# Beginning the first load from ScalarE's DMA queue instead of SyncE's

## The chip, the cores and the metric

The kernel runs on one core of a Trainium2 chip. A core has a matrix engine (TensorE, PE), three engines for elementwise work (VectorE or DVE, ScalarE or ACT, GpSimd or POOL) and SyncE (SP), which here only begins transfers. Transfers between the chip's memory and the core's on-chip memory are carried out by 16 DMA engines; an instruction on an engine's queue begins one. The metric is the device time of one execution in microseconds (us). Before the change the median of three runs is 224.49 us (224.32 to 224.66).

## The reference

Two blocks in a row, in float32. The first is a scan with decay: for 4 batches, 8 heads, 768 steps in chunks of 32, head width 32 and state width 16.

```python
log_a = np.log(np.clip(a, 1e-06, 1.0))
for c in range(nc):                       # chunks of 32 steps
    cum = np.cumsum(la, axis=-1)          # la: the chunk's log_a
    L = np.exp(cum[:, :, :, None] - cum[:, :, None, :]) * causal
    M = np.einsum('bhin,bhjn->bhij', Cc, Bc) * L
    y_intra = np.einsum('bhij,bhjd->bhid', M, xc)
    y_inter = np.einsum('bhin,bhnd->bhid', Cc, state) * np.exp(cum)[:, :, :, None]
    y[:, :, sl] = y_intra + y_inter
    state = decay_full[:, :, None, None] * state + np.sum(Bx, axis=2)
```

The second is a mixer on the result, laid out as 4 x 768 x 256: `u = x + (xt @ U @ V)` transposed back (rank 32, across the sequence), then `u + relu(u @ w_ch1) @ w_ch2` with 1024 hidden channels. U, V, w_ch1 and w_ch2 come in as float64 and are read as pairs of 32-bit words.

## The kernel before

The sequence of each batch is cut into three pairs of 128-step blocks, twelve pairs in all. One long hand-written list, PLAN, fixes the order of all steps on every engine; each word of it is a step and its numbers. In it, U0, B0, X0 and so on with a leading Y are loads begun early, A and K compute the decays, Q, T and V multiply and turn B and C, g, m and M make the masked products, n, j, i, s and u the scan itself, p and q the low-rank part, U, f, e, h and d the mixer's matmuls, c and R turn weight words into floats. F and the function `warm` put filler matmuls of the identity on TensorE (line 136), whose results nobody reads.

The kernel opens as follows. ScalarE loads the table of its activation functions (line 182). SyncE begins the load of `a` (line 186), 96 partitions of two rows of 512 bytes. Then helper constants are made on GpSimd and VectorE: the identity, triangles and the like (lines 301 to 332). TensorE runs a filler of 3 x 128 columns as soon as the identity is there, then turns `a` (line 343, `la_ps`), then another filler of 128 columns. VectorE clips the result (`la`, line 345), ScalarE takes its Ln (line 349). With the first words of PLAN, `YU0 c0 F3 YB0 A0 Q0.0 A1`, come the load of U's words, the start of their conversion, a filler of 3 x 128 columns, the first pair's B and C loads, and the decays: matmuls with `la` (lines 377 and 381), an Exp on ScalarE into F (line 384), and the product BC of B and C with F on VectorE (line 466, shown under the helper's line 174). F multiplies everything that follows.

All loads in PLAN go through `begin` (line 201), which uses the queue named by `issuer`. That is SyncE's queue, unless a word begins with Z, which then means ScalarE's; PLAN has no such word. SyncE works through its loads in order. Later ones (words B, X and w without a leading Y) are held until the last VectorE instruction written before them has ended (`hold`, line 194). The copy named `settled` (line 595) is a small VectorE instruction that keeps one group of matmuls behind another.

The diff touches the top level of the kernel's function. These are the lines in question, numbered as in the profile:

```python
182    nc.scalar.preload_act_table_set("natural_log_exp_and_others")
185    a_sb = const.tile([NB * NH * NC // 2, 2, P], FP32)
186    nc.sync.dma_start(
187        out=a_sb,
...
338    warm(3, "x")
343        nc.tensor.transpose(out=la_ps[:, g], in_=a_sb[:, g], identity=ident[:R, :R])
344    warm(1, "x")
```

Of the kernel before, what the change touches and what calls it, by code (L numbers as in the profile page):

```python
# [73 lines left out]
def kernel(  # L74
# [27 lines left out]
    nc = tc.nc  # L102
# [60 lines left out]
    class Kept:  # L163
# [6 lines left out]
        def __getattr__(self, name):  # L170
# [8 lines left out]
    vector = Kept(nc.vector)  # L179
    until = []  # L180

    nc.scalar.preload_act_table_set("natural_log_exp_and_others")


    a_sb = const.tile([NB * NH * NC // 2, 2, P], FP32)
    nc.sync.dma_start(
        out=a_sb,
        in_=a.rearrange("(g b) h (c s) -> g (b h c) s", g=2, s=P).rearrange(
            "g r s -> r g s"))

    x_sb, bc_sb = {}, {}
    pairs = [(b, q) for b in range(NB) for q in range(NPR)]
# [790 lines left out]
```

## Time and profile before

| | |
|---|---|
| median of 3 runs | 224.49 us (224.32 to 224.66) |
| the profiled execution | 224.41 us, of which the span from first to last instruction is 222.6 us |
| TensorE busy | 215.5 us (97%), 3022 matmuls |
| VectorE, ScalarE, GpSimd busy | 146.4, 108.7, 32.7 us |
| data moved | 14.59 MB by DMA, most of it in the first 60 us |
| issue of `a` on SyncE | at 0.81 us, 0.38 us long, landed 2.0 us after its start |
| issue of U's words on SyncE | at 1.24 us, 0.44 us long, landed 2.9 us after its start |
| ScalarE's table load | at 0.80 us, 1.28 us long |

In the rows of the profile, L186 is line 186 of the kernel, PE is TensorE's matmuls and PEld its weight loads, SPq the queue of SyncE's DMA instructions; `w<-ident,a_sb` means that the tile w is written from ident and a_sb, `x2` that two instructions are merged into the row. What stands in brackets is how long the engine was idle before it, and whose end released it. Ends of matmuls are modelled, their starts are recorded.

### The profile page before, as it was taken

What the parts mean: (1) busy time and instruction counts of PE and PEld (TensorE: products, weight loads), DVE (VectorE), ACT (ScalarE), POOL (GpSimd) and SP (SyncE); (2) the same over time, 40 slices, a digit from 0 to 9 for tenths busy, and PEclk for the clock granted to TensorE, in tenths of its full rate; (3) what the DMA queues carried; (4) which work ended last, traced back from release to release, by engine and by line L of the source; (5) the groups of instructions that cost most, each with busy time, mean ns of one, the idle gap of its engine ahead of it and who ended that gap; (6) DMA issues with size and microseconds to landing.
All of it is one profiled execution on the core that took longest, in us unless ns stands there. A gap on an engine that the chain in (4) does not pass through costs nothing.

```text
span 222.6 us, 7025 instructions
## 1 busy us (share of the span) xinstructions
PE 215.5 (97%) x3022; PEld 182.2 (82%) x3022; DVE 146.4 (66%) x314; ACT 108.7 (49%) x251; POOL 32.7 (15%) x44
## 2 busy tenths in 40 slices
PE   7999999999999999999999999999999999999994
PEld 4666566665668888889999996788999999999993
DVE  4688498568657755737955736959863955674921
ACT  3334745675668075543444214476535455553510
POOL 3012223405577053000010100000000000000000
PEclk9999999999999999999999999999999999999999
DMA  6968888898633446100120010000000100101011
GB/s 102 129 98 144 138 158 189 187 281 113 134 47 71 84 57 91 37 24 28 27 71 27 3 49 27 3 3 3 0 27 1 47 0 27 47 0 50 6 43 50
DMA packets 69520, 14.59 MB, mean 66 GB/s; under 512 B 63792, under 2 KB 67696, under 8 KB 69488
## 3 DMA queue, kind: packets, MB, share of 16 engines
q1 hardware_dynamic: 69488, 14.13, 32.3%
q8 instruction: 24, 0.39, 0.8%
q14 instruction: 8, 0.07, 0.1%
HBM read 10.98 MB, written 3.15 MB: 63 GB/s over the span
## 4 chain that ended last, share of the span: by engine, by line
PE 89%; DVE 5%; DMA 2%; SPq 2%; ACT 1%; issue 1%; POOL 0%; POOLq 0%
PE x L790 31%; PE z L790 24%; PE y L790 12%; PE y L680 3%; PE x L522 2%; PE y L642 2%; PE w L482 2%; DMA bc<-in_B_dram 2%; DVE M L174 2%; PE w L707 2%; SPq L202 2%; PE w L556 1%; PE x L136 1%; PE z L522 1%; PE w L734 1%; PE w L136 1%
## 5 line engine op out<-in xcount | busy, mean ns | idle before, releaser
L790 PE MATMUL z<-u,w 128*128 128x384 f32 x144 | 33.6, 347 | 0.0
L790 PE MATMUL x<-u,w 128*128 128x384 f32 x144 | 32.7, 344 | 0.5 <-DVE u L174 0.3
L174 DVE SCALAR_TENSOR_TENSOR words<-words 128x768 fp32r<-128x768 f32 (+3 forms) x35 | 29.5, 846 | 1.4
L790 PEld LDWEIGHTS x<-u,w 128*128 128x128 f32 x144 | 24.8, 188 | 1.8 <-DVE u L174 0.7
L795 ACT ACTIVATE x<-x 128x384 f32<-128x384 f32 (+1 forms) x30 | 13.6, 454 | 25.1 <-PE x L790 18.2
L790 PEld LDWEIGHTS z<-u,w 128*128 128x128 f32 x144 | 24.1, 189 | 0.9
L790 PE MATMUL x<-w2c,words 128*128 128x256 f32 x112 | 22.3, 339 | 0.0
L795 ACT ACTIVATE z<-z 128x384 f32<-128x384 f32 (+1 forms) x27 | 12.6, 466 | 18.6 <-PE z L790 18.6
L790 PE MATMUL y<-w,words 128*128 128x256 f32 x144 | 19.8, 283 | 0.0
L790 PEld LDWEIGHTS x<-w2c,words 128*128 128x128 f32 x112 | 18.3, 189 | 1.5
L174 DVE SCALAR_TENSOR_TENSOR words<-x,words 128x384 fp32r<-128x384 f32 x24 | 13.3, 554 | 9.3 <-ACT words L825 9.2
L790 PEld LDWEIGHTS y<-w,words 128*128 128x128 f32 x144 | 18.8, 190 | 0.3
L583 POOL TENSOR_TENSOR Sm<-S,own 128x256 f32<-128x256 f32 (+1 forms) x12 | 7.6, 634 | 76.4 <-DVE S L174 48.0
L174 DVE SCALAR_TENSOR_TENSOR words<-z,words 128x384 fp32r<-128x384 f32 x24 | 13.2, 552 | 5.2 <-ACT words L825 5.1
L825 ACT ACTIVATE words<-z 128x384 fp32r<-128x384 f32 x24 | 11.7, 491 | 10.1 <-PE z L790 10.0
L825 ACT ACTIVATE words<-x 128x384 fp32r<-128x384 f32 x24 | 11.8, 493 | 5.3 <-PE x L790 5.0
L790 PE MATMUL x<-w,words 128*128 128x256 f32 x96 | 14.2, 285 | 0.0
L790 PEld LDWEIGHTS x<-w,words 128*128 128x128 f32 x96 | 12.9, 190 | 0.2
L680 PEld LDWEIGHTS y<-M,x 64*32 64x32 f32 x768 | 8.1, 105 | 5.7 <-issue 3.0
L174 DVE TENSOR_TENSOR BC<-bc,F 128x512 f32<-128x512 f32 (+2 forms) x18 | 9.4, 535 | 4.7 <-DMA bc<-in_B_dram 3.2
L680 PE MATMUL y<-M,x 64*32 64x64 f32 x768 | 12.0, 223 | 0.4 <-DVE settled L174 0.3
L174 DVE SCALAR_TENSOR_TENSOR S<-S,kept,w 128x64 f32<-128x64 f32 x40 | 11.2, 279 | 1.6
(149 smaller groups left out, 411.9 us busy)
## 6 DMA issues: line engine op xcount, KB each, us to landing
words<-in_moe_w_ch_dram SPq DMA_DIRECT2D x7, 512.0 KB, 5.0
x<-in_x_dram SPq DMA_DIRECT2D x24, 128.0 KB, 3.7
out_dram<-ytok SPq DMA_DIRECT2D x24, 128.0 KB, 1.7
bc<-in_B_dram SPq DMA_DIRECT2D x24, 64.0 KB, 3.3
bc<-in_C_dram SPq DMA_DIRECT2D x12, 128.0 KB, 3.4
words<-in_moe_w_ch_dram SPq DMA_DIRECT2D x2, 256.0 KB, 3.8
words<-in_moe_U_dram SPq DMA_DIRECT2D x1, 192.0 KB, 2.9
words<-in_moe_V_dram SPq DMA_DIRECT2D x4, 48.0 KB, 2.8
```

What stands on the lines that cost most here:

```text
L136: nc.tensor.matmul(out=t[:, :m * P].rearrange("p (m i) -> p m i", i=P), lhsT=ident, rhs=ident[:, None, :].to_broadcast([P, m, P]), start=T ...
L174: self.last = call(*args, **kwargs)
L202: op = issuer[0].dma_start(**kwargs)
L482: nc.tensor.transpose(out=tp[:, i, v], in_=s["BC"][:, i, c + v].rearrange("p h n -> p (h n)"), identity=ident)
L522: nc.tensor.matmul(out=s["g"][r][cols, c], lhsT=s["T"][rows, 0, c, cols], rhs=s["Cm"][rows, :, :, ts(2 * c + p, Q)].rearrange("r v t i -> ...
L583: nc.gpsimd.tensor_tensor(out=s["Sm"][:, sl], in0=s["S"][:, sl].rearrange("p i (s d) -> p i s d", s=2), in1=own2[:, b, 4 * q + sl.start:4 ...
L642: behind["first"].append(nc.tensor.matmul(out=channels(k)[r // 2][ts(r % 2, H), c, p], lhsT=own[ts(r, Q)], rhs=st[k]["T"][ts(r, Q), 1, :, ...
L680: product = nc.tensor.matmul(out=y[n][ts(i, Q), c, p], lhsT=x_sb[k][half, c, h], rhs=s["M"][half, h // 2, c, h % 2], start=fresh(k, n, [i] ...
L707: nc.tensor.transpose(out=t[:, c, g], in_=yT[b][:, g, ts(2 * q + c, P)], identity=ident)
L790: nc.tensor.matmul(out=t, lhsT=lhsT, rhs=rhs, start=start, stop=True, skip_group_check=True)
L795: nc.scalar.activation(t, t, AF.Copy, scale=1.0 + EPS)
L825: nc.scalar.activation(gs[j, m // 2][0][:, m % 2], t, AF.Relu, scale=NEAR)
```

## The change

The load of `a` is begun by an instruction on ScalarE's queue, which stands ahead of ScalarE's table load. SyncE's queue, which had this load first, now begins with U's words. The order of all else on every engine is the same, and so are the data moved and the work computed.

```diff
-    nc.scalar.preload_act_table_set("natural_log_exp_and_others")
-
-
     a_sb = const.tile([NB * NH * NC // 2, 2, P], FP32)
-    nc.sync.dma_start(
+    nc.scalar.dma_start(
         out=a_sb,
         in_=a.rearrange("(g b) h (c s) -> g (b h c) s", g=2, s=P).rearrange(
             "g r s -> r g s"))
+
+    nc.scalar.preload_act_table_set("natural_log_exp_and_others")
```

## The prediction

> **What bounds the kernel now.** I read the page's busy shares first, then the timeline of the first 5 us with the DMA rows, then the chain of waits over the first 36 us, and last the rows where an engine waited for a load.
>
> From the head of the page, its busy times and its slices:
>
> ```profile
> span 222.6 us, 7025 instructions
> PE 215.5 (97%) x3022; PEld 182.2 (82%) x3022; DVE 146.4 (66%) x314; ACT 108.7 (49%) x251; POOL 32.7 (15%) x44
> PE   7999999999999999999999999999999999999994
> ```
>
> TensorE (PE) is busy for 215.5 of 222.6 us. All its idle time is 7.1 us, of which 1.43 us lies ahead of its first instruction. So a change that only hides work better can win little; one that makes PE wait early shifts all that follows.
>
> From the timeline of the first microseconds (start, length, what; in brackets the idle time before and its releaser), and then two rows of the DMA view (KB, median us from issue to landing):
>
> ```profile
> 0.80 1.28 ACT L182 ACT_TABLE_LOAD   x1 [0.80 <-PEq L967]
> 0.81 0.38 SPq L186 DMA_DIRECT2D a_sb<-in_a_dram  x1
> 1.24 0.44 SPq L202 DMA_DIRECT2D words<-in_moe_U_dram  x1
> 1.43 1.65 PE L136 MATMUL x<-ident 128*128 128x384 f32 x2 [1.43 <-POOL ident masks.py:199]
> 2.82 0.29 PEld L343 LDWEIGHTS w<-ident,a_sb 96*128 96x128 f32 x2 [0.89 <-DMA a_sb<-in_a_dram]
> 2.88 0.53 PE L343 MATMUL w<-ident,a_sb 96*128 96x96 f32 x2
> 3.98 0.36 ACT L349 ACTIVATE la<-la 128x192 f32<-128x192 f32 x1 [1.89 <-DVE la L174]
> ```
> ```profile
> words<-in_moe_U_dram SPq DMA_DIRECT2D x1, 192.0 KB, 2.9
> a_sb<-in_a_dram SPq DMA_DIRECT2D x1, 96.0 KB, 2.0
> ```
>
> The array a lands at 0.81 + 2.0 = 2.81, and its transposes start at 2.88, just when PE has done the filler matmuls of line 136. Both arrive together: an earlier a gives PE nothing, a later one makes it wait.
>
> From the chain of waits over the first 36 us:
>
> ```profile
> 1.43 1.65 PE x L136 x2
> 3.08 0.33 PE w L343 x2
> 3.40 0.48 PE x L136 x2
> 3.88 1.28 PE w L136 x2
> 5.16 0.64 PE w L377 x2
> ...
> 12.42 0.65 PE y L136 x2
> ...
> 19.61 4.09 DMA bc<-in_B_dram
> 23.70 0.02 issue
> 23.72 0.69 DVE BC L174
> 24.41 0.10 DVE settled L174
> ```
>
> Until 15 us the chain is PE, DVE and ACT, without a load after a; the first late load on it is a block of B, at 23.70. Two matmuls of 128x384 take 1.28 us at 3.88 and 0.65 us at 12.42: PE runs at half its pace at first, though the row of granted clocks shows 9 throughout.
>
> **The change part by part.** The sum is made against the profiled execution, 224.41 us: its span of 222.6 and 1.81 around it. It lies 0.08 under the median of the runs, 224.49.
>
> *Table load.* ACT and SP start within 0.01 us of each other (0.80, 0.81), so a's issue stays at about 0.80. I price it as SP's row: 0.38 us, and 0.43 to the next instruction (1.24 less 0.81). The table load moves to 1.23 and ends at 2.51. ACT's next work is the Ln at 3.98, which waits for DVE's la. That leaves 1.47 us of cover: cost nothing. Had the cover been under 0.43 us, the rest would have gone onto the chain through Ln.
>
> *a's landing.* What moves together with a changes. So far U's packets came behind a's, since U was issued 0.43 us later; now both queues start at once. In windows of 0.4 us from 1.80, 2.20 and 2.60 the DMA engines were 0.56, 0.59 and 1.01 busy at 159, 154 and 234 GB/s: while a moved, some 40% was free, and the full rate was 234. The best case is no delay (a still lands at 2.81; earlier is worth nothing). The worst is that U goes first and a lands only where U lands, 0.81 + 2.9 = 3.71: 0.9 late. Between them, with equal turns byte for byte, a's 96 KB go with 96 KB of U: 192 KB at 234 GB/s take 0.82 us, against 96 KB at about 157 GB/s, 0.61: 0.2 us late. I take 0.2, since the free share of the engines speaks for the near end.
>
> *What PE makes of it.* The cover is 0.06 us (weights at 2.82, matmul at 2.88); by the chain's modelled end of the fillers, 3.08, it would be up to 0.26. I take 0.06, as a start is measured and an end modelled. Behind the transposes PE has in its order the fillers at 3.40 and 3.88 and only then the decays of line 377, so these wait too although la is ready at 4.34: nothing there takes the delay up. After that the chain goes through ACT's Exp and DVE's BC, where PE's slow pace gives nothing back. So 0.2 - 0.06 = +0.14 us; ends 0 and +0.84.
>
> *SP's queue.* One issue goes: all SP loads may come up to 0.43 us earlier. The first one with a gate is the issue of w at 15.56, held by a BC product of DVE, which is done by about 15.2 (two of them run 14.94 to 15.56 and it is the first): so the lead past there is about 0.3, less what the delay of a takes from DVE. Who is waiting for these loads? No one before 20.52. From the timeline, the PE and DVE rows that wait for a load or follow it:
>
> ```profile
> 20.52 0.32 PE L556 MATMUL w<-x,BC 64*32 64x64 f32 x8 [0.26 <-DMA x<-in_x_dram]
> 23.72 0.69 DVE L174 TENSOR_TENSOR BC<-bc,F 128x512 f32<-128x512 f32 x1 [0.75 <-DMA bc<-in_B_dram]
> 23.76 0.45 PE L680 MATMUL y<-M,x 64*32 64x64 f32 x32
> 24.55 0.46 PE L680 MATMUL y<-M,x 64*32 64x64 f32 x32 [0.34 <-DVE settled L174]
> ```
>
> The wait at 20.52 is followed by one of 0.23 us for ACT's Vn at 21.07, so x earlier only lengthens the next wait. At 24.55 PE waits for the copy "settled", which stands behind BC on DVE but also waits for the products that PE ends at 24.21 (23.76 + 0.45); without the load it would start some 0.07 behind their end, as its copy at 19.09 does behind products ending at 19.02, so at 24.28 instead of 24.35. So 0.07 of the 0.34 is to be had. The DVE wait of 0.32 at 27.50 is covered, as its next M waits for PE's products ending at 28.6. I take -0.05. Ends: -0.60 (both waits of PE, 0.26 + 0.34, gone), and +0.8, as the landing of such a block differs by that much from load to load (4.09 on the chain, 3.3 in the median of B's loads), and a stream begun at another moment may fall worse; I stay near 0, since the block on the chain is already one of the late ones.
>
> *Around the span.* A second queue could cost at the end, where SP's queue waits 0.6 us in all for the other engines; ends 0 and +0.6, taken as 0, since ACT's own transfer is over 219 us before.
>
> Sum: 0.14 - 0.05 = +0.09 us: 224.50 for a run like the profiled one, and 224.6 beside the median of 224.49.
>
> **A page against it.** The windows show free DMA engines beside a, and the sum took equal turns from that. The Trainium skill, page "DMA: Bandwidth & Descriptors", section "Issuing engines are not separate DMA queues", says that starting transfers from several engines saves only the issuing time and that they interleave on the same engines; the section "Queues, rings and completion order" adds that the write that signals an end lands only after every earlier write of that engine, whatever its queue. By these, a's signal waits for U's packets that went ahead of it; in the extreme these are all of U's, and the sum would be 225.3, the first rival below, instead of 224.6. No run shown so far has two queues, so the trace decides nothing here.
>
> **The rivals.**
> - *a behind U (slower).* Place: the landing of a. The issue of U on SP is served first, or a's signal waits for U. a lands up to 3.71, PE waits 0.84: 224.49 + 0.84 - 0.05 = 225.3. It decides from a delay of about 0.55 on. For it: U has 768 pieces of 256 bytes against 192 of 512, and the engines are full from 2.6 on. Against: 40% free while a moves, and ACT starts 0.01 before SP. Chance 0.21.
> - *The loads' lead reaches PE (faster).* The waits at 20.52 and 24.55 both vanish: 224.49 - 0.60 = 223.9. It needs a to land in time, landings over 0.34 earlier, and ACT and DVE not to be next. Against: the rows of Vn and settled above. Chance 0.14, not all of it past the bound.
> - *The pace of PE (slower).* The half pace ends around 7 us. Should a gap at 2.9 put that off, the stretch from 7.2 to 11.0, with PE 3.39 us busy, would run at half pace: up to 3.4 us more, about half of it beside DVE's waits: 226.2. Against: PE is busy without a break from 3.1 to 7 in either case. Chance 0.04.
>
> **How the numbers follow.** My forecast, a small delay, has 0.61; its own range is 224.1 to 225.0. A measurement of this kernel can tell about 0.2% from no change, that is 0.45 us. Faster: 0.12 of the loads' lead and 0.01 of the forecast. Slower: 0.19 of a behind U, 0.04 of the pace and 0.06 of the forecast's own edge. The same holds 0.58. The range goes from 223.9 (the whole lead) to 225.4 (a behind U, a little over), leaving out the pace and part of the ends of the forecast.
>
> **What would show it.** In the changed profile: the issue of a on ACT's queue at 0.8 and the table load after it ending near 2.5; U issued at 0.8 on SP; a's time to landing (2.0 so far; 2.2 by my sum, 2.9 by the rival); the start of line 343 on PE (2.88 so far, 3.0 expected); the Ln about 0.14 later; the block of B near 23.70 landing up to 0.3 earlier with DVE's wait shorter and the PE row at 24.55 hardly moved. I am wrong if a lands where it did and PE still shifts, if ACT's issue takes much longer than SP's 0.38, or if the time moves by over 0.45 us with line 343 in its place: then it is in the loads after 15 us.

## The result and the profile after

The changed kernel takes 225.55 us in the median of four runs (225.35 to 225.68), the kernel before, now with a fourth run, 224.42 (224.32 to 224.66): a ratio of 1.0061, 95% interval 1.0046 to 1.0076. That is 1.13 us slower, where a time within 0.45 us of no change was held likeliest and 225.4 was the end of the range. The profiled execution took 225.48 us, 223.8 of it the span.

The timeline of the changed kernel's first microseconds, with the rows that answer to those shown of before (lines after 188 count one less than before):

```profile
0.80 0.45 ACTq L183 DMA_DIRECT2D a_sb<-in_a_dram  x1
0.81 0.42 SPq L201 DMA_DIRECT2D words<-in_moe_U_dram  x1
1.28 1.28 ACT L188 ACT_TABLE_LOAD   x1 [1.28 <-PEq L966]
1.43 1.65 PE L136 MATMUL x<-ident 128*128 128x384 f32 x2 [1.43 <-POOL ident masks.py:199]
4.12 0.29 PEld L342 LDWEIGHTS w<-ident,a_sb 96*128 96x128 f32 x2 [2.19 <-DMA a_sb<-in_a_dram]
4.12 0.58 PE L342 MATMUL w<-ident,a_sb 96*128 96x96 f32 x2 [1.05 <-DMA a_sb<-in_a_dram]
5.28 0.36 ACT L348 ACTIVATE la<-la 128x192 f32<-128x192 f32 x1 [2.71 <-DVE la L174]
```

And of its DMA view (KB, median us from issue to landing):

```profile
words<-in_moe_U_dram SPq DMA_DIRECT2D x1, 192.0 KB, 3.7
a_sb<-in_a_dram ACTq DMA_DIRECT2D x1, 96.0 KB, 3.3
```

The issue of a is where it was, at 0.80, but it lands 3.3 us later and no longer 2.0. TensorE has done its fillers at 3.08 and stands still for 1.05 us; the transposes begin at 4.12 instead of 2.88. U lands no earlier either: 0.81 + 3.7 = 4.5, against 1.24 + 2.9 = 4.1 before.

The chain of waits of the changed kernel shows what becomes of it:

```profile
0.80 3.27 DMA a_sb<-in_a_dram
4.08 0.05 issue
4.12 0.58 PE w L342 x2
4.70 0.48 PE x L136 x2
5.18 1.28 PE w L136 x2
6.46 0.64 PE w L376 x2
...
27.63 1.47 PE w L733 x12
...
33.46 1.53 PE z L789 x4
```

The last two rows stood in the chain of the kernel before as:

```profile
26.39 1.46 PE w L734 x12
...
32.22 1.53 PE z L790 x4
```

The chain now begins with the landing of a. The decays of the old line 377 start at 6.46 against 5.16 (1.30 later); the mixer's first matmuls of the old line 790 start at 33.46 against 32.22 (1.24 later); the span ends 1.2 later. TensorE's busy time is 215.5 us in both. So the whole loss is there after 4 us, and the rest of the kernel takes no more than about a tenth of a us of it back.

The packet records of the two traces part the 1.3 us of later landing. The end of a load is told by 16 signals, and it has landed with the last of them. Before, the first of a's 192 pieces of 512 bytes moved at 1.83 us, the last at 2.42, and the last signal came at 2.78. After, these are 2.24, 3.35 and 4.08. So 0.41 us is a later start, 0.52 (1.11 less 0.59) a slower run, and 0.37 (0.72 less 0.36) a later signal. U's first piece moved at 1.91: U, issued 0.01 us after a, was served before it. But a did not wait for all of U. Its first piece moved when 163 of U's 768 pieces had gone; then the two loads ran mixed, and a's last piece went before U's last (3.58), its last signal before U's (4.47).

### The profile page after: what moved, and what is told of

It reads as the page before. It is cut to its first block, busy times and chain, and to the rows that moved or that the text cites. A ratio compares the mean times of both kernels' runs of the same rounds, so it can differ in the third digit from the quotient of the medians.

```text
span 223.8 us, 7025 instructions
## 1 busy us (share of the span) xinstructions
PE 215.5 (96%) x3022; PEld 181.9 (81%) x3022; DVE 146.5 (65%) x314; ACT 108.6 (49%) x251; POOL 32.3 (14%) x44
## 4 chain that ended last, share of the span: by engine, by line
PE 91%; DVE 4%; DMA 1%; ACT 1%; issue 0%
PE x L789 31%; PE z L789 24%; PE y L789 12%; PE y L679 4%; PE y L641 3%; PE x L521 3%; PE w L481 2%; PE w L706 2%; PE w L555 2%; DMA a_sb<-in_a_dram 1%; DVE M L174 1%; PE z L521 1%; PE x L136 1%; PE w L733 1%; PE x L761 1%; PE w L751 1%
```

## The experiments

Two theories stood against each other at first: that U's load, begun at the same moment, holds a back (A), or that a first load from ScalarE's queue is slow in itself (B).

**U issued later.** The changed kernel, with U held until a small clearing on VectorE has ended:

```diff
     vector.memset(ref, 0.0)
+    until[:] = [vector.last]
```

> The changed kernel with one more wait: U's load on SyncE is held until VectorE has cleared a small tile (it ends near 1.2 us), so that U is issued near 1.27 us, about as in the kernel before, while a stays on ScalarE's queue at 0.80. Theory A, U's transfer, begun at the same moment, holds a back: a lands near 2.8 to 3.0 us (2.0 to 2.2 after its issue) and the time is 224.4 to 224.6. Theory B, a load begun from ScalarE's queue is slow in itself at this place: a lands near 4.0 us again (3.2 to 3.3 after its issue) and the time stays near 225.5.

The timeline of this kernel:

```profile
0.80 0.39 ACTq L183 DMA_DIRECT2D a_sb<-in_a_dram  x1
1.23 0.42 SPq L201 DMA_DIRECT2D words<-in_moe_U_dram  x1
2.95 0.29 PEld L343 LDWEIGHTS w<-ident,a_sb 96*128 96x128 f32 x2 [1.02 <-DMA a_sb<-in_a_dram]
2.95 0.58 PE L343 MATMUL w<-ident,a_sb 96*128 96x96 f32 x2
```

With U 0.43 us later, a lands at 2.91, its first piece moves at 1.84 (on SyncE's queue it was 1.83), and the time is 224.32 against 224.33 us (ratio 0.9998, 0.9989 to 1.0007). A load begun from ScalarE's queue starts as soon as one from SyncE's here; the loss is gone. Theory B falls. The wait delays the loads behind U on SyncE as well, so this run shows that SyncE's loads hold a back, and not whether U alone would do it: in the changed kernel 211 pieces of the block of B behind U also moved before a's last.

**U and then a, both on SyncE.** In the kernel before, the two loads change places:

```diff
-    nc.sync.dma_start(out=a_sb, ...)
...
+    load_u()
+    nc.sync.dma_start(out=a_sb, ...)
...
-    'YU0 c0 F3 ...
+    'c0 F3 ...
```

> Both loads on SyncE's queue, U first at 0.81 us and a behind it at about 1.25. It prices a behind U in one queue, without ScalarE's. If one queue serves its loads one after the other, a lands about where U landed as second load of the kernel before plus a little (U and a together were in at 4.15), so 3.7 to 4.1 us, and the time is 225.3 to 225.7, as in the changed kernel. If a lands near 3.2 us, 2.0 after its issue, then U ahead of it costs nothing and only the later issue counts, with 224.8.

Its timeline:

```profile
0.81 0.43 SPq L198 DMA_DIRECT2D words<-in_moe_U_dram  x1
1.29 0.53 SPq L297 DMA_DIRECT2D a_sb<-in_a_dram  x1
3.95 0.58 PE L344 MATMUL w<-ident,a_sb 96*128 96x96 f32 x2 [0.88 <-DMA a_sb<-in_a_dram]
```

One run, 225.25 us. Issued 0.49 us later and behind U in one queue, a still lands before it does in the changed kernel (at 3.91 against 4.08; weights at 3.95 against 4.12). U lands sooner too, at 3.58 against 4.47. A second queue did not bring a past U; both loads fared a little worse than in line. The first expectation, 3.7 to 4.1 for the landing, holds; its time is just under the 225.3 to 225.7 that went with it.

**Other loads in U's place.** Two kernels change only what SyncE begins with, while a is on ScalarE's queue; their times say little, since U's words come late in both.

```diff
-    'YU0 c0 F3 YB0 A0 ...  m1 YV0 Q2.0 ...
+    'YV0 YU0 c0 F3 YB0 A0 ...  m1 Q2.0 ...
```

> The changed kernel, with V's four loads (192 KB in 128 pieces of 1536 bytes) ahead of U's (192 KB in 768 pieces of 256) on SyncE, so that a on ScalarE's queue meets few large pieces instead of many small ones; U and all loads of B, C and x come some 1.9 us later, so the whole time says little here, only a's landing is read. If the number of pieces that SyncE's load puts in front holds a back, a lands near 2.8 to 3.1 us. If the bytes do it, a lands near 4 us as with U. Theory B, ScalarE's queue is slow in itself: near 4 us too.

```diff
-    'YU0 c0 F3 YB0 A0 ...
+    'YB0 YU0 c0 F3 A0 ...
```

> The changed kernel with the first pair's loads of B and C (1024 pieces each, of 64, 128 and 64 bytes) ahead of U's on SyncE. Only a's landing is read, since U's words come some 2 us later. U's 768 pieces of 256 bytes brought a to 4.08, V's 128 pieces of 1536 bytes to 3.09 for the same 192 KB. If the number of pieces in front counts, a lands as late as with U or later, 4.0 to 4.6. If the time that U's pieces take on the DMA engines counts (18 ns each against 11 for one of 64 bytes, 27 for one of a), a lands earlier than with U, 3.4 to 3.9.

The rows for a in the DMA views, first behind V's large pieces, then beside the small ones of B and C:

```profile
a_sb<-in_a_dram ACTq DMA_DIRECT2D x1, 96.0 KB, 2.3
```
```profile
a_sb<-in_a_dram ACTq DMA_DIRECT2D x1, 96.0 KB, 2.7
```

With V's pieces a lands at 3.09, with those of B and C at 3.51, with U's at 4.08 and, in a repeat, 4.25. V's 192 KB and U's are no fair pair, though: V comes as four loads of 48 KB, begun 0.45 us apart. What a really met is in the packet records, counted up to its last piece: 53 pieces of V's (80 KB), 953 of B's and C's (62 KB), 945 of U's and B's (197 KB). Bytes alone do not give the order of the landings, since B and C brought fewer than V and held a longer. Nor does the number of pieces alone, since 953 and 945 are all but the same. The time that these pieces took on the DMA engines, added up, does follow the order: 6.2, 10.0 and 15.3 us. Three runs are too few to make a rule of it. The start of a's first piece was late by about the same in all (2.13, 2.25, 2.24 against 1.84); what differs more is the run and the late signal. The times were 224.79 and 224.95 us, one run each.

**The price of the lead of SyncE's loads.** Here the kernel before is changed: a stays first on SyncE and U goes to ScalarE, so that SyncE's other loads can come 0.43 us earlier. The first form wrote only `ZU0` for `YU0` in PLAN.

> The kernel before, with U instead of a on ScalarE's queue, behind the table load, so issued near 2.1 us; a is first on SyncE at 0.81, and SyncE's other loads come 0.43 us earlier, as in the changed kernel. It prices the lead of SyncE's loads alone. Theory A: a lands at 2.8 us, the transposes start at 2.88, and the time is that of the kernel before less 0 to 0.1 us (the lead reaches no engine that sets the end), 224.3 to 224.45; U lands near 5, which ScalarE and VectorE can bear. A rival, the lead is worth the waits for x and B at 20.5 and 24.5: 223.8 to 224.0. Theory B adds that U takes clearly over 2.9 us to land.

It missed its aim. In the code U's load then stood behind the Ln on ScalarE and had to wait for the completion counter of an earlier load. The timeline and the chain:

```profile
10.20 0.48 ACTq L202 DMA_DIRECT2D words<-in_moe_U_dram  x1
```
```profile
6.83 3.35 DMA x<-in_x_dram
10.20 3.08 DMA words<-in_moe_U_dram
13.30 0.38 ACT words L424
13.67 0.24 ACT F L384
```

Issued at 10.20, U held ScalarE's conversion, and behind it the Exp that the decays need, and TensorE stood for 7 us: 233.55 us, ratio 1.0413 (1.0398 to 1.0427). The second form begins U's load right behind a's in the code:

```diff
     early = dict(loads, V=lambda n: load_v(), U=lambda n: load_u())
+    issuer[0] = nc.scalar
+    load_u()
+    issuer[0] = nc.sync
...
-    'YU0 c0 F3 ...
+    'c0 F3 ...
```

> The price of the lead of SyncE's loads alone, again: a first on SyncE, U on ScalarE's queue directly behind the table load (issued near 2.1 us, ahead of the Ln), so that every other load of SyncE comes up to 0.43 us earlier than in the kernel before, and no one meets a. My theory, that the lead reaches no engine that sets the end: a lands at 2.8, the transposes start at 2.9, the time is that of the kernel before within 0.15 us (ratio 0.9993 to 1.0007). The rival, that the lead takes away TensorE's waits near 20.5 and 24.5: 0.3 to 0.6 us less (ratio 0.9973 to 0.9987). U lands near 5 us; if ScalarE or VectorE then wait for it ahead of the decays, it could cost up to 0.3.

Its timeline:

```profile
0.81 1.28 ACT L182 ACT_TABLE_LOAD   x1 [0.81 <-PEq L970]
0.81 0.39 SPq L186 DMA_DIRECT2D a_sb<-in_a_dram  x1
0.84 0.48 ACTq L202 DMA_DIRECT2D words<-in_moe_U_dram  x1
1.25 0.44 SPq L202 DMA_DIRECT2D bc<-in_B_dram  x1
3.06 0.58 PE L346 MATMUL w<-ident,a_sb 96*128 96x96 f32 x2
```

U did not wait for the table load that stands before it: it was issued at 0.84, while the table was loading. So the two queues met again, with the roles exchanged, and this time a on SyncE was served first (first piece at 1.84, U's at 2.21) and lost only 0.24 us: it landed at 3.02. The time is 224.58 against 224.22 us, ratio 1.0018 (1.0005 to 1.0030). SyncE's first loads of B, C and x were issued 0.2 to 0.6 us earlier and nothing was won; the gain of 0.3 to 0.6 that the rival expected is excluded, and the 0.15 either way of the author's own theory is missed as well. The loss is 0.36, with the transposes only 0.19 later. The profile shows where part of the rest comes from: the chain passes through a late block of B,

```profile
22.94 4.73 DMA bc<-in_B_dram
```

and TensorE, 0.17 us ahead of the kernel before at 28 us, starts the mixer 0.16 behind it (32.38 against 32.22). What made the block late, and the rest of the loss, is open.

**How much of a lead a needs.** The changed kernel with U held until a tile of ones is written, in a single run and then in twelve:

```diff
     vector.memset(ones, 1.0)
+    until[:] = [vector.last]
```

> The changed kernel with U's issue held until a tile of ones is written, so at about 1.1 us, between the 0.81 of the changed kernel (a landed at 4.08) and the 1.23 of the first experiment (2.91). Theory A1, order of service: a load whose issue is 0.3 us ahead has its pieces made first and U's follow; a lands at 2.9 to 3.1. Theory A2, sharing in proportion to the overlap: a lands near 3.3 to 3.6. By either, TensorE's transposes start with the landing, and the time follows it to 0.2 us.

> The changed kernel with U held to about 1.1 us, timed: a landed at 2.81 there, as in the kernel before, and SyncE's loads come 0.14 us earlier than in the kernel before. If the loss is a's landing alone, all of it is gone: ratio to the kernel before 0.998 to 1.001. If a first load from ScalarE's queue costs something in itself, it is still over 1.002. The one look gave 223.76, which lies inside the spread of the kernel before on that chip (223.65 to 224.95); if it was no chance, the ratio is near 0.998.

The timeline of the single run:

```profile
1.10 0.43 SPq L201 DMA_DIRECT2D words<-in_moe_U_dram  x1
2.85 0.29 PEld L343 LDWEIGHTS w<-ident,a_sb 96*128 96x128 f32 x2 [0.92 <-DMA a_sb<-in_a_dram]
```

And that of one of the twelve:

```profile
1.09 0.43 SPq L201 DMA_DIRECT2D words<-in_moe_U_dram  x1
3.04 0.29 PEld L343 LDWEIGHTS w<-ident,a_sb 96*128 96x128 f32 x2 [1.10 <-DMA a_sb<-in_a_dram]
```

A lead of 0.3 us restores the landing (2.81 in the one, 3.00 in the other). The median of twelve is 224.15 against 224.34 us, ratio 0.9997 (0.9984 to 1.0010). Of the two theories order of service fits this landing, and sharing in proportion does not.

The single run's 223.76 has another source than a's landing. Its trace shows the same two rows of TensorE, here first from the kernel before and then from this run:

```profile
4.96 0.85 PE L377 MATMUL w<-la,ref 128*128 128x192 f32 x2
8.10 0.49 PE L392 MATMUL z<-la,middle 128*128 128x192 f32 x2
```
```profile
4.99 0.68 PE L377 MATMUL w<-la,ref 128*128 128x192 f32 x2
7.62 0.49 PE L392 MATMUL z<-la,middle 128*128 128x192 f32 x2
```

The decays start 0.03 us later than before, and the row at line 392 starts 0.48 earlier. In between TensorE goes from half pace to full pace: the record of the full clock begins at 7.12 us in the kernel before and at 5.36 here.

**Both queues for a.** A try for a kernel better than both, made from the changed one: each half of a on a queue of its own, the first filler shorter by a block.

```diff
-    nc.scalar.dma_start(out=a_sb, ...)
+    for g, queue in enumerate((nc.sync, nc.scalar)):
+        queue.dma_start(out=a_sb[:, g], ...)
...
-    warm(3, "x")
+    warm(2, "x")
```

> A try for a faster kernel: a in two loads of 48 KB at the same moment, one on SyncE and one on ScalarE ahead of its table load, U behind the first on SyncE at about 1.25 us, and the first filler on TensorE cut from 3 to 2 blocks of 128 columns. If two queues carry a faster than one, its second half lands at 2.5 to 2.7 and TensorE's chain starts 0.15 to 0.35 us earlier: 224.0 to 224.2 beside 224.35. If all pieces go through one maker in turn, the two halves land where the one load did, 2.8 to 3.0, and the time is unchanged within 0.2.

Its timeline:

```profile
2.68 0.35 PEld L343 LDWEIGHTS w<-ident,a_sb 96*128 96x128 f32 x2 [0.75 <-DMA a_sb<-in_a_dram]
```

The halves landed at 2.64 (SyncE) and 2.81 (ScalarE, whose first piece moved at 1.96 against 1.83), and TensorE's chain began 0.19 us earlier than before. The time did not follow: 224.31 against 224.22 us, ratio 1.0010 (0.9995 to 1.0025). In its profile the chain passes through a block of B that lands late, as before, 4.47 us after its issue:

```profile
19.60 4.47 DMA bc<-in_B_dram
...
32.62 1.53 PE z L790 x4
```

The mixer starts at 32.62, against 32.22 before. In this profile TensorE is still 0.15 us ahead of the kernel before at 23 us, and 0.41 behind it after that block. So the landing of one such block can cost more than a start 0.19 us earlier brings. No kernel tried here beats the kernel before by more than can be measured.

**The changed kernel again, and a issued late.** The last two ask whether the order of service is a matter of chance, and whether the time follows a's landing whatever made it late.

> The changed kernel once more, unaltered, timed beside the two kernels below on one chip. If the loss is that of a's landing, 1.0 to 1.4 us over the kernel before, and a lands at 4.0 to 4.1 again, 1.2 to 1.3 late, with ScalarE's issue at 0.80 and SyncE's at 0.81. If the order in which two issues at the same moment are served were a matter of chance, a would land near 2.9 in some runs, and the runs would fall in two groups about 1.2 us apart.

Six runs lie between 225.65 and 226.27, in one group: 226.07 against 224.34 us, ratio 1.0079 (1.0064 to 1.0093). In its profile the issues are at 0.80 and 0.81 again, a lands at 4.25 and the transposes start at 4.30. Landing and loss (1.73) are both past what was expected (4.0 to 4.1, and 1.0 to 1.4). The order looks like no chance: SyncE's load went first in all six profiles in which the two queues began together.

```diff
-    nc.scalar.dma_start(out=a_sb, ...)
...
     for v in range(2):
         ...
         vector.tensor_tensor(out=ref[half, half], ...)
+        if v == 0:
+            hold(nc.scalar.dma_start(out=a_sb, ...), vector.last)
```

> The changed kernel with a's issue, still on ScalarE's queue, but behind the table load and held until a small VectorE product has ended, at about 2.2 us; SyncE's loads are those of the changed kernel, U first at 0.81. Here a is late because it is issued 1.4 us later. My theory, that the time follows a's landing whatever made it late: a lands at 4.3 to 5.0 (2.1 to 2.8 after its issue, amid the loads of B and C), TensorE's transposes start with it, and the time over the kernel before is that delay less 0 to 0.3 us: 1.2 to 2.1. If the loss were in the meeting of the two queues at 0.8 and not in the landing, the time would be under 0.6 us over the kernel before.

The timeline:

```profile
5.60 0.46 ACTq L320 DMA_DIRECT2D a_sb<-in_a_dram  x1
8.50 0.58 PE L343 MATMUL w<-ident,a_sb 96*128 96x96 f32 x2 [5.42 <-DMA a_sb<-in_a_dram]
```

Its issue came at 5.60 and not at 2.2: it counts its end on the same completion counter as a block of B begun at 2.49, and was issued only when that block had landed, at 5.52 (the chain has this landing just before it). That makes the test stronger: the transposes start 5.62 us later than before, and the time is 230.05 against 224.34 us, 5.71 more.

Here are all kernels with more than one run, except the one in which ScalarE's conversion waited for U; the starts are those of the profiled execution, the time is the difference of the medians:

| kernel | transposes start | full clock from | line 392 starts | time over before |
|---|---|---|---|---|
| the kernel before | 2.88 | 7.12 | 8.10 | |
| a in two halves | 2.69 | 6.32 | 7.95 | +0.09 |
| U held to 1.23 | 2.95 | 5.87 | 7.89 | -0.01 |
| U held to 1.1 | 3.04 | 6.11 | 8.03 | -0.19 |
| U on ScalarE | 3.06 | 5.98 | 7.99 | +0.36 |
| the changed kernel | 4.12 | 7.99 | 9.40 | +1.13 |
| the same again | 4.30 | 9.42 | 9.68 | +1.73 |
| a issued late | 8.50 | 11.55 | 13.48 | +5.71 |

The time follows a's landing, to within 0.4 us. Part of what is left over can be seen in the traces. The same work lies between the start of the decays and line 392 in all of these; it takes 2.63 us where the full clock comes 0.37 us after the decays' start (the single run above), and 3.25 where it comes 2.99 after (the changed kernel again), and the others lie between in the same order. Another part is the late blocks of B: in the changed kernel's repeat one lands 4.42 us after its issue, and TensorE falls a further 0.2 behind there. How these two fell in the runs without a profile is not known.

## Why the prediction was wrong

It named the right place and the right chain, and sized one term far too small: the delay of a's landing.

- *a's landing* is the step that failed: "Between them, with equal turns byte for byte, ... 0.2 us late. I take 0.2". It was 1.3 late. Equal turns assumed that both loads begin together and share the engines by bytes. The packets show that U's were served first (0.41 us), that a's then ran at half their pace (0.52), and that the signal came later behind the last piece (0.37). The middle part alone is over the whole 0.2: while a ran, 156 KB of SyncE's loads moved beside its 96, and not 96. The free share of the DMA engines, "0.56, 0.59", was read as room for both. These are the windows of the kernel before, and then those of the changed one (the last two numbers are the share of the DMA engines and GB/s):

```profile
1.80:2.20 0.40, 0.40 (x1) 0.13 (x1) 0.28 (x2) 0.29 (x1) 0.32 (x2) 1.00 0.56 159
2.20:2.60 0.40, 0.40 (x2) 0.00 (x0) 0.39 (x2) 0.00 (x0) 0.00 (x0) 1.00 0.59 154
2.60:3.00 0.40, 0.40 (x2) 0.18 (x2) 0.20 (x1) 0.00 (x0) 0.13 (x1) 1.00 1.01 234
```
```profile
1.80:2.20 0.40, 0.40 (x1) 0.13 (x1) 0.29 (x2) 0.40 (x1) 0.30 (x2) 1.00 0.39 92
2.20:2.60 0.40, 0.40 (x2) 0.00 (x0) 0.39 (x2) 0.36 (x1) 0.00 (x0) 1.00 0.54 129
2.60:3.00 0.40, 0.40 (x1) 0.00 (x0) 0.20 (x1) 0.00 (x0) 0.14 (x1) 1.00 1.17 301
```

  The engines were not even as full as before while a waited; what a lacked was its turn. Nor was 234 GB/s "the full rate": the changed kernel moves 301 from 2.60 on. With that rate the term would have come out smaller still, so it is not what made it too small.
- *The worst case* of that step, "0.81 + 2.9 = 3.71", was no bound. It took U's landing from a run in which U met nothing. Here U itself needed 3.7, and a's signal came at 4.08. So the range ended at 225.4, a little under the result.
- *The rival "a behind U"* was the case that came true, with 225.3 and a chance of 0.21: U was served first. But its picture, a landing where U lands, is only half right. a was in before U; both were slowed by each other, and a came 0.37 us past the bound of 3.71. That the sum preferred the near end rested on the free engines and on ScalarE's start 0.01 us earlier; neither decided the order of service here.
- *The pages weighed against it* were right in direction. The Trainium skill, page "DMA: Bandwidth & Descriptors", section "Queues, rings and completion order", has the end's signal wait for earlier writes of the same engine from any queue; the later signal (0.72 us behind the last piece, 0.36 before) agrees with it, though no experiment took it apart from the rest.
- *What PE makes of it* was right: a cover of 0.06 us and everything behind it shifted. The transposes start 1.25 late for a landing 1.30 late, and the run with 5.62 later costs 5.71.
- *The table load* was right at no cost: it ended at 2.56, and the Ln then waited 2.71 us for la.
- *SP's queue* was priced at -0.05 with ends of -0.60 and +0.8. The kernel with that lead and a nearly in time showed no gain (+0.36, with 0.19 of it from a). The rival in which the lead reaches PE did not come true. The 0.07 that was to be had at 24.55 did not show either. In the changed profile the block of B is in earlier and DVE's wait for it shrinks from 0.75 to 0.21, but PE still waits 0.34 for "settled": the copy now waits for PE's products and starts 0.14 behind their end (25.59 against 25.45), no sooner than it did before (24.35 against 24.21).
- *Around the span* nothing was added: 225.48 - 223.8 = 1.7 us, against 1.8 before.
- *The pace of PE*, the third rival, did not make the loss: in the changed profile the full clock came at 7.99, 0.87 us later than before for work 1.30 later, and the shift is 1.30 at the decays and 1.30 at line 392. That was partly luck, since the moment differs from run to run: in the repeat it came at 9.42 and cost 0.1 us more, and in the kernels with U held it gave back 0.3 to 0.5. The sum took one moment for granted.

## What to carry to other kernels

A load that everything waits for should begin alone: another queue does not give it a way of its own, and a load of many small pieces begun at the same moment can cost it more than standing in line would (here a landed at 4.08 and 4.25, against 3.91 in the one run in line). A head start of 0.3 us was enough here, and the second queue then did no harm, but no good either. When a transfer's neighbours change, its landing time is no longer the row of the old profile, and the worst case must include that the neighbour is slowed as well. Before a few tenths of a us between two profiles are put down to a change, compare when TensorE came to full pace in each.

## What was not expected of the hardware

- When SyncE and ScalarE issued within 0.03 us of each other, SyncE's load was served first in all six profiles, also when ScalarE's issue came 0.01 us earlier. The first piece of a from ScalarE's queue came 0.1 us (beside the other half of a) to 0.4 us later than alone.
- A DMA issue on ScalarE's queue did not wait for the table load ahead of it: the load was issued at 0.84 while the table load ran from 0.81 to 2.09. By this, putting the load of a ahead of the table load or behind it should make next to no difference to when it begins.
- The moment at which TensorE goes from half to full pace differed much from run to run, by the records of the granted clock, and the same kernel had it at 7.99 and 9.42 us. Where TensorE stood for about 0.9 us or more ahead of the transposes it came at 7.36, 7.99, 9.42 and 11.55, and at 7.65 where it stood for 0.47; where it hardly stood there, between 5.05 and 6.78 in seven profiles, but at 7.12 in the kernel before. So the gap may put it off, but it is not the whole of it, and the runs do not show what else sets it.
- After TensorE had stood for 7 us, in the kernel whose U was issued at 10.20, the records show the half clock again from 10.20 to 17.02, while its work began again at 13.95.
